# Weight preparation moved from GpSimd to VectorE, and a normalisation moved from the attention to the blocks' loads

## The chip, the cores and the metric

The kernel runs on one core of a Trainium2 chip. The metric is the device time of one execution in microseconds. Three executions of the kernel before took 843.49, 842.67 and 841.82 us; their median is 842.67 us. Engines are named as the profile names them: PE is TensorE (PEld its weight loads), DVE VectorE, ACT ScalarE, POOL GpSimd, and SP the engine that issues most transfers.

## What is computed

Three layers follow one another. The retention attention has 4 sequences of 576 tokens, 8 heads of 64. Its output, 2,304 tokens by 512 features, goes through a gated MLP with a root-mean-square normalisation in front, and the MLP's output goes to one of 8 experts per token, chosen by the first maximum of eight logits.

```python
scores = scale * q @ k.T;  ret = scores * Dmat          # Dmat[h,i,j] = gamma[h]**(i-j) for i >= j, else 0
x = (ret @ v).transpose(0, 2, 1, 3).reshape(2304, 512)
rms = sqrt(mean(x * x, -1) + 1e-6);  xn = x / rms * rms_g
y = silu(xn @ w_gate) * (xn @ w_val) @ w_out            # 512 -> 1536 -> 512
logits = y @ gate + modality_bias[modality_id]
out = softmax(logits)[e] * (relu(y @ w1[e]) @ w2[e])    # e = argmax, 512 -> 1024 -> 512
```

The gated MLP's weights arrive as 64-bit floating-point words. Each is brought to float32 and split into a high and a low part, and each product of the MLP is three matmuls (high by high, high by low, low by high).

## The kernel before, in words

The order of the work is written out by hand: each engine runs its instructions in the order in which the program emits them, and a tile's buffers (`bufs=`) are handed on when their last reader or writer is done.

**Attention** (lines 224 to 456). It goes in 20 steps, 5 chunks per sequence: four of 128 tokens and one of 64. In step g the loop of line 402 emits the loads of chunk g + 7 on SP, the decay of the next chunk's v on POOL (line 274), the scores of chunk g on PE (285) and their mask on DVE (289, two instructions), the sum of squares of chunk g − 3 on PE (348) with its square root on ACT (353), the state update (304, copied by ACT at 309 and 310), and the output of chunk g − 1 on PE (317 from the state, 324 from the chunk itself). DVE scales the output into the tile `x` (334), ACT squares it (336), and POOL adds the four squares of each token in two steps (338, 339). Four steps behind, `a_norm2` takes the reciprocal of the root on DVE (359) and multiplies x by it (360). Six steps behind, `a_store` (364) writes x to `xnd` in memory. The first 512 tokens, chunks 0 to 3, do not go through memory: `split_x` (198) splits them into the high and low parts of block 0 in steps 7 to 10 (DVE line 201, four instructions per chunk). The last three chunks stay in the tile `xlate` and are normalised and stored in steps 4 to 6 of block 0.

**Weight preparation.** `unpack` (127) treats one unit of 128 by 512 words in three stages. Stage 0 loads the raw words on SP (131). Stage 1 scales the low words on ACT (136), shifts the high words on DVE (137), merges two bit fields on DVE (140), and adds both as integers on POOL (143). Stage 2 rounds to the high part on ACT (147) and subtracts for the low part (148), on POOL or DVE as `lo_eng` says. `pipe` (174) staggers the units: a tick runs stage 1 of unit i, stage 2 of unit i − 2, and the load of a later unit. Five units are prepared in the attention from step 11 on, all on POOL. The other 30, with one more in two halves, are prepared beside block 0, three or four ticks a step, with `lo_eng` POOL for every second one.

**Gated MLP** (lines 735 to 848). Its blocks have 512, 512, 384, 384, 256 and 256 tokens, each in 12 steps of 128 hidden features. A step is 24 matmuls of gate and value (`gv_mm`, 212), the product on ACT and DVE (`gv_post`, 741: line 745 silu on ACT, 746 on DVE, 747 on ACT, 748 on DVE), and 3 matmuls for each chunk of the block (12 for four chunks) of the output projection of the step before (`out_acc`, 751). In block 0 the ticks of the weight preparation stand behind `gv_post`, so that in block 0 DVE runs lines 746 and 748 of a step and then that step's three or four units. A unit is needed by PE one or two steps later. `load_x` (187) brings the next block's x from `xnd` into the one buffer `xl`, in step 8 of block 0 and in step 2 of the others; at the end of a block `split_x` splits it. In blocks 1 to 5 DVE also routes the block before: line 767 forms a logit, with its unwanted products written to a corner of the tile `xl`.

**Experts** (line 850 to the end) are the same in both kernels.

Of the kernel before, what the change touches and what calls it, by code (L numbers as in the profile page):

```python
# [7 lines left out]
F32 = mybir.dt.float32  # L8
# [16 lines left out]
# tokens of the gated MLP's blocks: the first one hides the weight preparation, the last ones shorten the routing  # L25
# [3 lines left out]
NS0 = BLOCKS[0] // 128  # chunks that go to the first block without a trip to memory  # L29
XW = max(BLOCKS[1:])  # L30
CHUNKS = [(c * 128, min(128, S - c * 128)) for c in range(-(-S // 128))]
ROW = 528  # row of the experts' lists: features, logits, token
CAPS = [512, 512, 384, 320, 256, 256, 256, 256]  # static places by rank of an expert's count
EARLY = 256  # places of the first expert that are visited before the last block is routed
FILL = 512  # places of each list that are cleared
NL = 32  # most chunks beyond the static places
NWU = 13  # matmuls that wake the tensor engine's clock
QB = 8  # attention inputs in flight
XB = 10  # attention outputs in flight
SD = 6  # steps from an attention output to its store  # L40
# [15 lines left out]
def kernel(  # L56
# [39 lines left out]
    xnd = dram.tile([KD, 128, NT], F32, name="xnd")  # L96
    xs = dram.tile([E * NT, ROW], F32, name="xs")

# [1077 lines left out]
```

## Time and profile before

| What | us |
|---|---|
| median of three executions | 842.67 (841.82 to 843.49) |
| span of the profiled execution | 840.5 |
| PE busy | 802.7 (96%) |
| DVE busy | 523.0 (62%) |
| ACT busy | 291.1 (35%) |
| POOL busy | 181.7 (22%) |

The page gives the profiled execution as a span, from its first to its last instruction; the times of the executions are some 2 us longer. PE's busy time is an upper bound of its work, since matmuls overlap in the array and their ends are modelled. The start of one group of instructions to the start of the next is the safer measure of what a group takes. Shares over the whole span mix stages with different limits, so the stages have to be read one by one.

### The profile page before, as it was taken

The page shows a single profiled execution, that of the slowest core. Times are in us where ns is not written, and L with a number is a line of the kernel's source. Part 1 is how long each engine was busy: PE and PEld are TensorE (multiplying, and loading weights), DVE is VectorE, ACT ScalarE, POOL GpSimd, SP SyncE. Part 2 cuts the span into 40 slices and gives each one's busy share as a digit, 9 for nine tenths or more (in the row PEclk, how much of TensorE's full clock was granted, in tenths as well). Part 3 has the DMA queues.
Part 4 walks back from the last instruction along what each step waited for, and adds up shares of the span by engine and source line. Part 5 has one row for each costly group of instructions (what it writes and reads, how often), then busy time and mean ns, then how long its engine had stood idle before and what let it go on. Part 6 is the DMA issues. An engine that isn't in the chain of part 4 may idle for free.

```text
span 840.5 us, 13238 instructions
## 1 busy us (share of the span) xinstructions
PE 802.7 (96%) x5004; PEld 693.7 (83%) x5004; DVE 523.0 (62%) x1142; ACT 291.1 (35%) x567; POOL 181.7 (22%) x203
## 2 busy tenths in 40 slices
PE   8978988888999999999999999999999999999995
PEld 6867766656888889999999999999888898889894
DVE  3999799997454525654644475836575556576650
ACT  5443544344311113113111312124453344455540
POOL 4556766767000000010000001000100010011100
PEclk9998999999999999999999999999999999999998
DMA  9994463437930001000000100032635254776400
GB/s 322 338 328 169 148 246 109 134 109 253 325 129 27 1 13 51 15 26 14 26 14 13 32 21 26 14 130 110 212 142 189 89 194 149 271 265 226 147 19 12
DMA packets 47537, 106.29 MB, mean 126 GB/s; under 512 B 11182, under 2 KB 20398, under 8 KB 47344
## 3 DMA queue, kind: packets, MB, share of 16 engines
q1 hardware_dynamic: 43248, 95.32, 34.0%
q0 software_dynamic: 3168, 9.59, 3.0%
q8 instruction: 40, 0.66, 0.3%
q10 hardware_dynamic: 1056, 0.52, 0.2%
q14 instruction: 25, 0.20, 0.1%
HBM read 83.51 MB, written 22.82 MB: 127 GB/s over the span
## 4 chain that ended last, share of the span: by engine, by line
PE 77%; DVE 14%; issue 4%; DMA 2%; ACT 2%; POOL 1%; SPq 0%; another core or an unknown queue 0%; POOLq 0%; ACTq 0%; DVEq 0%
PE gv L208 10%; PE gv L210 10%; PE gv L209 10%; PE acc L208 10%; PE acc L209 9%; PE acc L210 9%; PE h L208 4%; PE h L209 4%; PE h L210 4%; DVE rawbt L137 3%; DVE rawbt L140 2%; DVE pt L289 2%; DVE w L148 1%; PE tp L723 1%; DVE x L360 1%
## 5 line engine op out<-in xcount | busy, mean ns | idle before, releaser
L210 PE MATMUL gv<-xh,w 128*128 128x512 f32 (+2 forms) x576 | 195.3, 339 | 7.9 <-POOL w L148 7.9
L208 PE MATMUL gv<-xh,w 128*128 128x512 f32 (+2 forms) x576 | 196.2, 341 | 2.6 <-ACT scratch L745 2.6
L209 PE MATMUL gv<-xo,w 128*128 128x512 f32 (+2 forms) x576 | 194.5, 338 | 0.0
L210 PEld LDWEIGHTS gv<-xh,w 128*128 128x128 f32 x576 | 109.3, 190 | 18.9 <-POOL w L148 11.1
L208 PEld LDWEIGHTS gv<-xh,w 128*128 128x128 f32 x576 | 109.5, 190 | 12.1 <-ACT scratch L745 3.0
L746 DVE TENSOR_TENSOR scratch<-gv,scratch 128x512 f32<-128x512 f32 (+2 forms) x72 | 40.0, 556 | 126.5 <-PE gv L210 126.5
L209 PEld LDWEIGHTS gv<-xo,w 128*128 128x128 f32 x576 | 109.4, 190 | 9.5
L747 ACT CAST hh<-scratch 128x512 fp32r<-128x512 f32 (+2 forms) x72 | 37.0, 514 | 177.2 <-DVE scratch L746 177.2
L676 DVE TENSOR_TENSOR w<-raw,w 128x1024 fp32r<-128x1024 f32 x64 | 78.1, 1225 | 26.1 <-ACT w L675 25.5
L767 DVE CUSTOM_DVE_ANT_0 xl<-row,wr 128x512 bf16<-128x512 f32 x128 | 88.2, 689 | 4.8 <-DMA xl<-xnd 2.2
L208 PE MATMUL h<-xt,w 128*128 128x256 f32 (+3 forms) x288 | 88.8, 308 | 0.0
L209 PE MATMUL acc<-wo,hh 128*128 128x512 f32 x216 | 85.6, 396 | 2.9 <-POOL wo L148 2.9
L208 PE MATMUL acc<-wo,hh 128*128 128x512 f32 x216 | 86.1, 399 | 2.3 <-ACT hh L747 2.3
L518 POOL DMA_INDIRECT xs<-row,sloti x16 | 18.0, 1127 | 320.8 <-DVE lg L767 173.6
L210 PE MATMUL h<-xt,w 128*128 128x256 f32 (+3 forms) x288 | 87.3, 303 | 0.0
L209 PE MATMUL h<-xt,w 128*128 128x256 f32 (+3 forms) x288 | 87.2, 303 | 0.0
L210 PE MATMUL acc<-wo,hl 128*128 128x512 f32 x216 | 85.6, 396 | 0.0
L745 ACT ACTIVATE scratch<-gv 128x512 f32<-128x512 f32 (+2 forms) x72 | 35.3, 491 | 143.5 <-PE gv L210 138.5
L893 POOL DMA_INDIRECT out_dram<-orow,idx x22 | 23.6, 1074 | 218.6 <-ACT ex L700 76.2
L748 DVE TENSOR_TENSOR hl<-scratch,hh 128x512 fp32r<-128x512 f32 (+2 forms) x72 | 40.8, 567 | 41.8 <-ACT hh L747 41.8
L675 ACT CAST w<-raw 128x1024 fp32r<-128x1024 f32 x64 | 66.0, 1043 | 1.5 <-DMA raw<-in_w_dram 1.5
L208 PE MATMUL acc<-w,rh 128*128 128x512 f32 (+1 forms) x160 | 63.6, 397 | 0.0
(216 smaller groups left out, 1352.7 us busy)
## 6 DMA issues: line engine op xcount, KB each, us to landing
raw<-in_w_dram SPq DMA_DIRECT2D x64, 512.0 KB, 4.9
rawb<-in_wgv_dram SPq DMA_DIRECT2D x20, 512.0 KB, 3.9
xs<-zero SPq DMA_DIRECT2D x8, 1056.0 KB, 13.3
qk<-in_qkt_dram SPq DMA_DIRECT2D x16, 512.0 KB, 7.9
vk<-in_vkn_dram SPq DMA_DIRECT2D x16, 512.0 KB, 9.4
rawb<-in_wout_dram SPq DMA_DIRECT2D x10, 512.0 KB, 3.6
rowc<-xs SPq DMA_DIRECT2D x19, 264.0 KB, 4.3
xnd<-x SPq DMA_DIRECT2D x8, 256.0 KB, 3.1
```

Source lines behind the costliest of these rows:

```text
L137: DVE.tensor_scalar(out=u, in0=hw, scalar1=3, scalar2=0x3FFFFFF8, op0=ALU.logical_shift_left, op1=ALU.bitwise_and)
L208: PE.matmul(ps, lh, rh, start=start, stop=False)
L209: PE.matmul(ps, lh, rl, start=False, stop=False)
L210: PE.matmul(ps, ll, rh, start=False, stop=stop)
L675: ACT.copy(out=w[:, 0, :], in_=raw)
L676: DVE.tensor_tensor(out=w[:, 1, :], in0=raw, in1=w[:, 0, :].bitcast(F32), op=ALU.subtract)
L745: ACT.activation(out=h, in_=gps[:, :n], func=ACTF.Silu)
L746: DVE.tensor_tensor(out=h, in0=vps[:, :n], in1=h, op=ALU.mult)
L747: ACT.copy(out=hh[:, :n], in_=h)
L748: DVE.tensor_tensor(out=hl[:, :n], in0=h, in1=hh[:, :n].bitcast(F32), op=ALU.subtract)
L767: DVE.tensor_tensor_reduce(out=junk, in0=row[:, 0:DM].rearrange("p (a b) -> p a b", a=2), in1=wr[:, e, :].rearrange("p (a b) -> p a b", a= ...
L893: POOL.indirect_dma_start(out=out[:, :], out_offset=bass.IndirectOffsetOnAxis(ap=idx[:m, i:i + 1], axis=0), in_=orow[:m, :], in_offset=Non ...
```

## The change

The weight preparation leaves POOL: lines 143 and 148 run on DVE for all units, and `lo_eng` is gone. The chunks behind the first block (4 to 19) are no longer normalised in the attention. They are stored as they come, three steps behind their output instead of six, all within the attention. Their sums of squares are gathered in four groups of 448 tokens (chunks 4 to 7, 8 to 11, 12 to 15, 16 to 19), one matmul and one square root per group, and the row of roots goes to a new array `rmsd` in memory. Each block loads its x one step (or, in block 0, five steps) away from where it did, in step 3, together with its row of roots spread over all partitions; from step 5 on DVE takes two reciprocals (half the tokens each) and two products (two of the four feature groups each), one instruction a step. In block 0 that row sits in the space of the router's weights `wr`, in the others in a row tile. The last chunk's sum of squares goes through POOL like the others. Comments were removed too.

```diff
-XB = 10  # attention outputs in flight
-SD = 6  # steps from an attention output to its store
+XB = 7
+SD = 3
-NLX = 3  # attention outputs normalised beside the first block
-LN = (4, 5, 6)  # the steps of the block that do so
-LP = 1  # last steps whose squares are summed on the tensor engine
+FX, FN = (3, 3), (5, 5)
+    rmsd = dram.tile([1, NT], F32, name="rmsd")
-    def unpack(src, hi, lo, raw, t, lo_eng):
+    def unpack(src, hi, lo, raw, t):
...
-            POOL.tensor_tensor(out=u, in0=u, in1=lw, op=ALU.add)
+            DVE.tensor_tensor(out=u, in0=u, in1=lw, op=ALU.add)
...
-            lo_eng.tensor_tensor(out=lo(), in0=u.bitcast(F32), in1=hi().bitcast(F32), op=ALU.subtract)
+            DVE.tensor_tensor(out=lo(), in0=u.bitcast(F32), in1=hi().bitcast(F32), op=ALU.subtract)
+    def norm_x(j, xl, rl):
+        t0, n = STARTS[j], BLOCKS[j]
+        rl = rl[:, :n]
+        SP.dma_start(out=rl, in_=rmsd[0:1, t0:t0 + n].to_broadcast([128, n]))
+        def inverse(o):
+            DVE.reciprocal(out=rl[:, o:o + n // 2], in_=rl[:, o:o + n // 2])
+        def scale(k):
+            DVE.tensor_tensor(
+                out=xl[:, k:k + 2, :n], in0=xl[:, k:k + 2, :n], in1=rl.unsqueeze(1).to_broadcast([128, 2, n]),
+                op=ALU.mult,
+            )
+        return [lambda: inverse(0), lambda: inverse(n // 2), lambda: scale(0), lambda: scale(2)]
...
-            if g < G - NLX:
-                x = att.tile([128, NP, 128], F32, tag="x", name="x", bufs=XB)
-            else:
...
+            x = att.tile([128, NP, 128], F32, tag="x", name="x", bufs=XB)
...
+            total = sq[:, 0, :n]
+            if g >= NS0:
+                gr, o = place[g]
+                if not o:
+                    sums[gr[0]] = att.tile([128, 512], F32, tag="sqs", name="sqs", bufs=2)
+                total = sums[gr[0]][:, o:o + n]
+            POOL.tensor_tensor(out=sq[:, 0:2, :n], in0=sq[:, 0:2, :n], in1=sq[:, 2:4, :n], op=ALU.add)
+            POOL.tensor_tensor(out=total, in0=sq[:, 0, :n], in1=sq[:, 1, :n], op=ALU.add)
...
         def a_norm1(g):
+            n, sq = steps[g][3], sq_t.pop(g)[:, 0, :]
+            if g >= NS0:
+                gr, o = place[g]
+                if g != gr[-1]:
+                    return
+                n, sq = o + n, sums.pop(gr[0])
+            ss = ps_g("ss")
+            PE.matmul(ss[:, :n], ones, sq[:, :n], start=True, stop=True)
...
+            if g < NS0:
+                ri_t[g] = ri
+            else:
+                b, c, o, _ = steps[gr[0]]
+                t0 = b * S + o
+                (ACT if g == G - 1 else SP).dma_start(out=rmsd[0:1, t0:t0 + n], in_=ri[0:1, :n])
...
-            q = ACT if G - NLX - LS <= g < G - NLX else SP
+            q = ACT if g >= G - LS else SP
...
-            if g >= NL2:
+            if NL2 <= g < NL2 + NS0:
                 a_norm2(g - NL2)
...
-                if j == 0 and f in LN:
-                    a_norm2(G - NLX + LN.index(f))
-                if j == 0 and f - 1 in LN:
-                    a_store(G - NLX + LN.index(f - 1))
-                if f == (LN[-1] + 2 if j == 0 else 2) and j + 1 < NB:
+                if f == FX[min(j, 1)] and j + 1 < NB:
                     x_in[:] = [load_x(j + 1)]
+                    norm = norm_x(j + 1, x_in[0], row_tile(F32, "rl") if j else wr[:, 0, :])
+                if j + 1 < NB and 0 <= f - FN[min(j, 1)] < len(norm):
+                    norm[f - FN[min(j, 1)]]()
```

## Rows read from the trace of the kernel before

**Rows 1.** Busy us by stage: PE, PEld, DVE, ACT, POOL; PE clock, DMA share, GB/s.

```profile
6.00:42.00 36.00, 34.47 (x511) 29.59 (x511) 26.10 (x40) 19.79 (x52) 19.42 (x25) 1.00 1.03 348
42.00:95.50 53.50, 42.96 (x557) 36.27 (x555) 51.63 (x82) 22.66 (x58) 32.92 (x39) 0.93 0.70 219
95.50:104.00 8.50, 8.50 (x39) 7.07 (x38) 4.71 (x7) 4.66 (x9) 7.38 (x7) 0.84 0.60 207
104.00:202.00 98.00, 82.30 (x338) 62.06 (x337) 90.54 (x98) 43.12 (x76) 65.37 (x42) 0.99 0.46 151
212.00:640.00 428.00, 427.96 (x2421) 380.90 (x2421) 234.39 (x693) 111.38 (x219) 29.13 (x56) 1.00 0.21 72
```

**Rows 2.** Waits of PE, 20 to 212 us: total, times, longest.

```profile
PE gv L210 <- POOL w L148: 7.9, 6, 1.9
PE st L304 <- POOL vk L274: 5.5, 6, 3.0
```

**Rows 3.** Timeline of PE, step 8 of the attention: start, us, line, operation.

```profile
34.38 1.16 PE L285 MATMUL sc<-qk 64*128 64x128 f32 x16
35.48 0.49 PE L348 MATMUL ss<-sq,ones 128*128 128x128 f32 x2
35.89 0.69 PE L304 MATMUL st<-vk 128*64 128x64 f32 x16
36.51 1.16 PE L317 MATMUL pv<-qk,sbd 128*128 128x128 f32 x8
37.60 1.09 PE L324 MATMUL pv<-pt,vk 128*64 128x128 f32 x16
38.62 0.68 PE L285 MATMUL sc<-qk 64*64 64x64 f32 x16
```

**Rows 4.** Timeline of DVE, step 7 of the attention and the start of step 8.

```profile
33.23 1.28 DVE L289 TENSOR_TENSOR pt<-sc,causal 128x512 f32<-128x512 f32 x2
34.50 0.69 DVE L334 TENSOR_TENSOR x<-pv,rc 128x512 f32<-128x512 f32 x1
35.11 0.94 DVE L359 RECIPROCAL ri<-ri 128x128 f32<-128x128 f32 x1
36.09 1.20 DVE L360 TENSOR_TENSOR x<-x,ri 128x512 f32<-128x512 f32 x1
37.22 2.11 DVE L201 SCALAR_TENSOR_TENSOR xo<-x,gt,xh 128x128 fp32r<-128x128 f32 x4
39.25 1.28 DVE L289 TENSOR_TENSOR pt<-sc,causal 128x512 f32<-128x512 f32 x2
```

**Rows 5.** Timeline of PE, the first matmul of block 0.

```profile
95.47 0.79 PE L208 MATMUL gv<-xh,w 128*128 128x512 f32 x1
```

**Rows 6.** Timeline of DVE in block 0: first step, a contended subtraction, tenth step.

```profile
103.73 0.69 DVE L746 TENSOR_TENSOR scratch<-gv,scratch 128x512 f32<-128x512 f32 x1 [3.73 <-PE gv L210]
...
105.72 0.42 DVE L137 TENSOR_SCALAR rawbt<-rawb 128x512 int32<-128x512 int32 x1
106.18 0.69 DVE L140 SCALAR_TENSOR_TENSOR rawbt<-rawb,rawbt 128x512 int32<-128x512 int32 x1
106.79 0.42 DVE L137 TENSOR_SCALAR rawbt<-rawb 128x512 int32<-128x512 int32 x1
...
110.97 0.68 DVE L148 TENSOR_TENSOR w<-rawbt,w 128x512 fp32r<-128x512 f32 x1
...
122.72 1.75 DVE L148 TENSOR_TENSOR w<-rawbt,w 128x512 fp32r<-128x512 f32 x1
...
202.27 0.68 DVE L746 TENSOR_TENSOR scratch<-gv,scratch 128x512 f32<-128x512 f32 x1
```

**Rows 7.** Groups by line, block 0, POOL's integer add: busy us, mean ns.

```profile
L143 POOL TENSOR_TENSOR rawbt<-rawbt,rawb 128x512 int32<-128x512 int32 x29 | 43.8, 1511 | 32.3 <-ACT rawb L136 12.4 <-DVE rawbt L140 9.2 <-ACT scratch L745 4.6
```

**Rows 8.** Timeline of POOL beside the contended subtraction of DVE.

```profile
122.21 1.71 POOL L148 TENSOR_TENSOR w<-rawbt,w 128x512 fp32r<-128x512 f32 x1
```

**Rows 9.** Waits of SP's queue, 0 to 215 us: total, times, longest.

```profile
SPq L131 <- POOL rawbt L143: 79.7, 21, 7.8
```

More of the change, by code (lines that the diff above doesn't have):

```diff
@@ L160, in once, with gv_unit @@
         return get
-    def gv_unit(u, raw, t, lo_eng):
+    def gv_unit(u, raw, t):
         f, i = divmod(u, 2)
@@ L170, in part @@
             return get
-        return unpack(wgv[f, i], part(0), part(1), raw, t, lo_eng)
+        return unpack(wgv[f, i], part(0), part(1), raw, t)
     def pipe(units, lead=2):
@@ L250 @@
         qk_t, vk_t, pt_t, x_t, sq_t, ri_t = {}, {}, {}, {}, {}, {}
-        late = []
+        groups, sums = [], {}
+        for g in range(NS0, G):
+            n = steps[g][3]
+            if not groups or sum(steps[i][3] for i in groups[-1]) + n > 512:
+                groups.append([])
+            groups[-1].append(g)
+        place = {g: (gr, sum(steps[i][3] for i in gr[:z])) for gr in groups for z, g in enumerate(gr)}
         def by_pair(ps):
@@ L336, in a_pv @@
             ACT.activation(out=sq[:, :, :n], in_=x[:, :, :n], func=ACTF.Square)
-            if g < G - LP:
-                POOL.tensor_tensor(out=sq[:, 0:2, :n], in0=sq[:, 0:2, :n], in1=sq[:, 2:4, :n], op=ALU.add)
-                POOL.tensor_tensor(out=sq[:, 0, :n], in0=sq[:, 0, :n], in1=sq[:, 1, :n], op=ALU.add)
+            total = sq[:, 0, :n]
[6 more added lines that the diff above has]
+            POOL.tensor_tensor(out=total, in0=sq[:, 0, :n], in1=sq[:, 1, :n], op=ALU.add)
             x_t[g], sq_t[g] = x, sq
         def a_norm1(g):
-            n = steps[g][3]
-            ss = ps_g("ss") if g < G - 2 else ps_o("ss")
-            sq = sq_t.pop(g)
-            parts = 1 if g < G - LP else NP
-            for p in range(parts):
-                PE.matmul(ss[:, :n], ones, sq[:, p, :n], start=(p == 0), stop=(p == parts - 1))
-            if g < G - NLX:
+            n, sq = steps[g][3], sq_t.pop(g)[:, 0, :]
[7 more added lines that the diff above has]
+            if g < NS0:
                 ri = att.tile([128, 128], F32, tag="ri", name="ri", bufs=3)
             else:
-                ri = late[0][:, g - G + NLX, NLX * 128:NLX * 128 + 128]
+                ri = att.tile([128, 512], F32, tag="rig", name="rig", bufs=2)
             ACT.activation(out=ri[:, :n], in_=ss[:, :n], func=ACTF.Sqrt, scale=1.0 / DM, bias=eps[:, 0:1])
-            ri_t[g] = ri
+            if g < NS0:
+                ri_t[g] = ri
[3 more added lines that the diff above has]
+                (ACT if g == G - 1 else SP).dma_start(out=rmsd[0:1, t0:t0 + n], in_=ri[0:1, :n])
         def a_norm2(g):
@@ L372, in unit_a @@
             t = once(lambda: att.tile([128, DM], I32, tag="rawt", name="rawt", bufs=3))
-            return gv_unit(u, raw, t, POOL)
+            return gv_unit(u, raw, t)
         def wo_unit_a():
@@ L378, in wo_unit_a @@
             wo[0] = w = once(lambda: w4_tile([128, 2, DM], F32R, "wo", True))
-            return unpack(wout[0], lambda: w()[:, 0, :], lambda: w()[:, 1, :], raw, t, POOL)
+            return unpack(wout[0], lambda: w()[:, 0, :], lambda: w()[:, 1, :], raw, t)
         prep_a = pipe([unit_a(u) for u in range(NUA)] + [wo_unit_a()], LD)
@@ L448 @@
                 split_x(x_t.pop(g - SX), xsp, 128 * (g - SX), 128)
-        for g in range(G + 1 - SD, G - NLX):
+        for g in range(G + 1 - SD, G):
             a_store(g)
@@ L472, in unit_b @@
         if kind == "gv":
-            return [gv_unit(u, raw, t, lo_eng)]
+            return [gv_unit(u, raw, t)]
         w = once(lambda: w4_tile([128, 2, DM], F32R, "wo"))
@@ L476, in unit_b @@
             wo[u] = w
-            return [unpack(wout[u], lambda: w()[:, 0, :], lambda: w()[:, 1, :], raw, t, lo_eng)]
+            return [unpack(wout[u], lambda: w()[:, 0, :], lambda: w()[:, 1, :], raw, t)]
         wo[u] = w
@@ L484, in unit_b @@
                 wout[u, :, i:i + 256], lambda i=i: w()[:, 0, i:i + 256], lambda i=i: w()[:, 1, i:i + 256],
-                raw, t, lo_eng,
+                raw, t,
             ))
@@ L784 @@
         ulist = []
-        for i, (kind, u) in enumerate(units):
-            ulist += unit_b(kind, u, POOL if i % 2 else DVE)
+        for kind, u in units:
+            ulist += unit_b(kind, u)
         prep_b = pipe(ulist)
```

5 lines of the change are left out of this document (1 added, 4 removed).

## The prediction

> **What bounds the kernel now.** I read the busy time by stage first [rows 1]. It shows three stages. From 42 to 95.5 us (the second half of the attention) and from 104 to 202 us (the first block of the gated MLP) DVE is busy 51.6 of 53.5 and 90.5 of 98 us while PE has holes; from 212 us on PE is busy 427.96 of 428 us. So time can be won only ahead of 212 us, and there only by work taken from DVE, or from whatever DVE waits for. The waits say the same of PE [rows 2]: its two longest waits are for POOL, 5.5 us for the decayed v of the attention and 7.9 us for weights' low parts, and POOL's one queue holds the weight preparation in both stages. Then the two chains in the attention: PE's own work of a full step takes 38.62 − 34.38 = 4.24 us, of which the sum of squares is 0.41 [rows 3]; DVE's of the step before it, with a normalisation and a split for block 0, 39.25 − 33.23 = 6.02 us [rows 4]. PE needs 8.26 us from the first matmul of block 0 to DVE's first product there [rows 5, 6], at a granted clock of 0.84, and DVE then needs 202.27 − 103.73 = 98.5 us for nine steps of the block [rows 6].
>
> **The change, part by part.** I go from stage to stage, with start-to-start times.
>
> Attention, steps 8 to 20. Removed from DVE: the reciprocal (0.98) and the multiply (1.13) of each chunk from 4 on [rows 4]. Steps 4 to 7 keep them, so nothing moves up to 39.25 us, when DVE starts the mask multiply of step 8. From there a step of DVE is mask 1.27 + output 0.61 + split 2.03 while the splits last (steps 8 to 10): 3.9 + 3.3 (64 tokens: half the mask) + 3.6 (half the output) gives 50.1. Steps 11 to 19 are mask and output: six full at 1.88, the two of 64 tokens at 1.26 and the one behind the first of them at 1.57, 15.4 us. Into them come five weight units. Each takes on DVE the shift 0.46 and the merge 0.61 as now, and new an integer add and a subtraction. The subtraction is 0.60 as DVE's own [rows 6]. The add is on no row of DVE: below it stands 0.46 (one int32 input, same shape), above it 1.51, which POOL takes for it [rows 7]. I take 0.61, that of the merge, which also reads two int32 tiles of this size on DVE. Four and a half units of 2.28 are 10.3 us. 50.1 + 15.4 + 10.3 = 75.8; the routing constants, unchanged, come on top, for which I put 3 (an estimate: one and a half full steps' masks and outputs), about 79.
>
> PE over the same time: the mask of step 10 ends at 39.25 + 3.9 + 3.3 + 1.27 = 47.7 and its output matmuls (1.02) at 48.7. Steps 12 to 20 are six full ones (3.83 without the sum of squares), less 1.09 where a sequence begins, half the scores and half an output at each chunk of 64 tokens, and two group sums of 448 columns (between 0.41, one chunk, and 1.44, 3.5 chunks; I take 1.0): 30.4 us, so 79.1. The transfers: 36 × 348 GB/s and 53.5 × 219 GB/s moved 24.2 MB from 6 to 95.5 us, and three chunks' stores (0.64 MB) come in from block 0; at 348 GB/s that is 71 us, to about 77. Three chains near 79 will not pass without stops: where PE and DVE were close, PE lost 1.5 of 36 us [rows 1], which is 1.6 of these 40.
>
> Here row and rule part. DVE's subtraction took 0.68 at 110.97 us and 1.75 at 122.72 us [rows 6], 1.07 more; the second one ran beside a subtraction of POOL that had begun at 122.21 us [rows 8]. The attention keeps POOL busy with decays and sums, and nine adds and subtractions on two inputs come to DVE there; if each met POOL, 9.6 us; at a quarter of them, 2.4. So 79 + 1.6 + 2.4 = 83 for the end of the attention, between 79 and 90, where 95.5 stood. The Trainium skill (SBUF — State Buffer, Who interferes with whom) says that a DVE instruction with two SBUF inputs and a GpSimd instruction that reads SBUF lock each other out for a whole instruction. By that rule the move pays in block 0, where POOL falls idle, and costs in the attention; the sum by it alone would take the 90.
>
> The stores come three steps after the output instead of six, and three more of them, with three of the four root-mean-square rows, are issued by SP inside the attention. What stands behind them on SP is the raw weights. SP spent 79.7 us waiting for raw tiles that POOL held [rows 9]; that wait covers the issues. Without it, raw weights land late, ACT's conversion and DVE's shift wait, and the masks queued behind them: a part of the 90.
>
> Entry of block 0: 8.26 us at a clock of 0.84 are 7.0 at full clock, if PE's holes behind POOL are gone; the group's sum takes the place of the single chunks' sums. DVE's first product comes at 83 + 7 = 90.0 instead of 103.7. It also waits for ACT, which now issues the last stores and the last row ahead of the block's activation: nothing while two passes of matmuls hide it, otherwise about a microsecond.
>
> Block 0, nine steps of DVE: product to first shift 105.72 − 103.73 = 1.99 [rows 6], nine times 17.9; 30 units' shift, merge and add 1.68 each, 50.4; 28 subtractions 16.8; the next block's normalisation, two reciprocals of 256 columns at 1.96 (twice 128) and two products of 1,024 elements at 1.2 (twice the subtraction), 6.3. Together 91.4 against 98.5, bounds 86 (add 0.46, half the normalisation) and 95 (a POOL-free price of the add 0.12 higher). Three late chunks' normalisation, some 5 us, is what the 6.3 replaces. So the tenth product stands at 181.4 instead of 202.3, and PE, which then has 72 matmuls of the block ahead of it as before, ends 20.9 us earlier. PE's own nine steps are about 36 matmuls each and shorter (it had 82.3 busy of 98 us), so DVE still sets the pace.
>
> Blocks 1 to 4. Four normalisations of the block after come to DVE, four instructions each, and a load of x one step later with a row spread over the partitions beside it on SP. Priced as above, 384 columns cost 4.7 and 256 cost 3.2: 15.8 us in all, against 234 of 428 us busy [rows 1]. I cost them at nothing, covered by PE's one step of lookahead; without cover they are 15.8 us.
>
> The sum is −13.7 − 7.1 = −20.8: span 840.5 becomes 819.7. The median, 842.67, is 2.2 above the profiled span; I keep that and predict 822.0.
>
> **The rivals.** *Contention and late raw weights take the attention's part.* For: DMA at a share of 1.03 up to 42 us [rows 1] and the 1.75 beside 0.68. Against: only nine such instructions. The attention ends at 90, the gain is 13.8, and the time 829. The Trainium skill's rule of the shared ports (SBUF — State Buffer, Who interferes with whom) would be the mechanism; the trace's 1.75 agrees with it, and no run shows yet how often it strikes in the attention.
>
> *Slower: the integer add is dear on DVE.* It decides in block 0, where DVE has no slack: each 0.1 us more costs 3 us in 30 units. At 0.61 + 20.8/30 = 1.30 all is given back; at POOL's 1.51 the loss is 27 of which 20.8 are paid, 842.67 + 6 = 849. For: no row shows it. Against: the merge, two int32 inputs, at 0.61.
>
> *The normalisation stalls the later blocks.* For: it is queued on DVE ahead of the products that PE waits for, and the blocks of 256 tokens give it the shortest steps to hide in. If half of 15.8 us came through, 830. Against: PE has no hole from 212 to 640 us [rows 1].
>
> *No gain*: raw weights, not DVE, become the pace of both stages, so that the time stays at 842. Against: in block 0 DMA has a share of 0.46 [rows 1].
>
> **How the numbers follow.** The forecast, DVE relieved in both stages, has 0.72. Contention has 0.10, stalls in later blocks 0.06, no gain 0.05, the dear add 0.07. The forecast's own bounds: 79 for the attention and 86 for the block give −30 and 812; 90 and 95 give −10.2 and 832. The range 813 to 833 takes in the first three cases but for their edges, about 0.82. Faster by over 0.2% (1.7 us, about what a measurement of this kernel can tell from no change) is the sum of these three, 0.88; same 0.05; slower 0.07.
>
> **What would show it.** Right: the first product of block 0 near 90 us and the tenth near 181; POOL without work from there to the block's end; shift, merge, add and subtraction at 0.4 to 0.7 each; PE without waits for POOL's weights; PE still full from 190 us on. Wrong: an add far above 0.7, which overthrows block 0; subtractions and adds near 1.7 in the attention, or ACT and DVE waiting there for raw tiles, which overthrows the 83; holes of PE behind DVE in the blocks of 384 and 256 tokens, which overthrow the zero. If DVE reached 79 as summed and PE did not, the term that failed is the handing over between them.

## The result and the profile after

The changed kernel takes 832.65 us, the median of four runs (831.01 to 836.12); the kernel before took 843.08 on the same chip (841.82 to 846.14). The ratio is 0.9876, with a 95% interval of 0.9857 to 0.9895: 10.4 us faster where 20.7 were forecast. The profiled execution took 832.61 us with a span of 830.8.

Busy time by stage of the changed kernel, columns as in [rows 1], with the edges moved to where its stages now begin:

```profile
6.00:42.00 36.00, 34.10 (x505) 28.95 (x504) 25.16 (x38) 19.03 (x49) 19.35 (x24) 1.00 1.02 336
42.00:86.00 44.00, 37.76 (x540) 31.23 (x536) 35.24 (x66) 20.38 (x48) 24.94 (x33) 1.00 0.92 290
86.00:97.00 11.00, 8.71 (x34) 6.18 (x30) 4.57 (x9) 5.75 (x9) 2.88 (x4) 0.84 0.81 291
97.00:194.00 97.00, 84.86 (x348) 64.98 (x346) 85.66 (x141) 42.27 (x76) 0.00 (x0) 0.98 0.45 146
212.00:640.00 428.00, 427.96 (x2425) 381.33 (x2424) 247.78 (x710) 109.20 (x216) 29.89 (x56) 1.00 0.19 67
```

The second half of the attention shrank from 53.5 to 44 us; DVE is busy 35.2 of those 44 and no longer fills them, while the DMA share rose from 0.70 to 0.92. The entry of block 0 (86 to 97) got longer, with the clock still at 0.84. In block 0 POOL has no work at all. Behind 212 us PE is as full as before (427.96 of 428) with 13.4 us more of DVE beside it: the later blocks' normalisation costs nothing, as forecast.

Waits of PE (total, times, longest), first from 42 to 97 us, then from 97 to 194; they answer to [rows 2]:

```profile
PE st L327 <- POOL vk L297: 3.4, 3, 1.4
PE ss L374 <- POOL sqs L362: 3.1, 2, 2.3
...
PE acc L224 <- ACT hh L778: 6.8, 4, 2.3
PE acc L225 <- DVE wo L147: 4.3, 4, 1.5
```

The wait for POOL's weights is gone, and in block 0 PE waits for ACT and DVE instead; the wait for the decayed v is not gone, and POOL's sum of squares now stands in the entry.

DVE in the attention of the changed kernel (start, us, line, operation, idle time before it); it answers to [rows 4]:

```profile
42.47 2.47 DVE L217 SCALAR_TENSOR_TENSOR xo<-x,gt,xh 128x128 fp32r<-128x128 f32 x4 [1.38 <-ACT xh L216]
...
47.19 2.47 DVE L217 SCALAR_TENSOR_TENSOR xo<-x,gt,xh 128x128 fp32r<-128x128 f32 x4 [0.99 <-ACT xh L216]
...
52.02 2.06 DVE L217 SCALAR_TENSOR_TENSOR xo<-x,gt,xh 128x128 fp32r<-128x128 f32 x4 [0.83 <-ACT xh L216]
...
65.32 0.69 DVE L352 TENSOR_TENSOR x<-pv,rc 128x512 f32<-128x512 f32 x1 [2.00 <-PE pv L347]
65.92 0.17 DVE L470 CAST mf<-m 128x18 f32<-128x18 int32 x1
```

In [rows 4] the split follows the normalisation without idle time. With the normalisation gone, DVE comes to the split before ACT has its rounded part: 1.38 + 0.99 + 0.83 = 3.2 us of waits in steps 8 to 10. The last two lines (output of step 13, then the routing mask's cast, which finds its load landed) are taken up below.

The entry of block 0, timelines of PE, ACT and DVE; it answers to [rows 5, 6]:

```profile
86.11 0.51 PE L224 MATMUL gv<-xh,w 128*128 128x512 f32 x1
...
91.46 1.73 PE L374 MATMUL ss<-sqs,ones 128*128 128x448 f32 x2 [2.29 <-POOL sqs L362]
92.31 1.31 PE L224 MATMUL gv<-xh,w 128*128 128x512 f32 x1
...
93.23 0.63 ACT L379 ACTIVATE rig<-ss,eps 128x448 f32<-128x448 f32 x1 [1.99 <-PE ss L374]
...
94.40 1.28 ACT L776 ACT_TABLE_LOAD   x1 [0.54 <-ACT rig L379]
95.70 0.60 ACT L776 ACTIVATE scratch<-gv 128x512 f32<-128x512 f32 x1
...
96.97 0.69 DVE L777 TENSOR_TENSOR scratch<-gv,scratch 128x512 f32<-128x512 f32 x1 [5.00 <-PE gv L226]
```

From first matmul to first product 10.86 us, where 8.26 stood and 7.0 was forecast. PE runs out of matmuls at 89.2 and waits for the last chunk's sum. Ahead of the wait its granted clock is 1.00 (86.0 to 89.2) and a matmul's record is 0.39 to 0.40 long; behind it the clock is 0.51, near the lower level of 1.2 GHz, until 95.1, and three full records there are 0.63 long.

One weight unit of block 0 on DVE, and the tenth product; it answers to [rows 6]:

```profile
109.77 0.42 DVE L136 TENSOR_SCALAR rawbt<-rawb 128x512 int32<-128x512 int32 x1
110.22 0.69 DVE L139 SCALAR_TENSOR_TENSOR rawbt<-rawb,rawbt 128x512 int32<-128x512 int32 x1
111.05 0.69 DVE L142 CUSTOM_DVE_ANT_0 rawbt<-rawb,rawbt 128x1024 uint16<-128x1024 uint16 x1
111.66 0.68 DVE L147 TENSOR_TENSOR wo<-rawbt,wo 128x512 fp32r<-128x512 f32 x1
112.26 0.42 DVE L136 TENSOR_SCALAR rawbt<-rawb 128x512 int32<-128x512 int32 x1
...
193.96 0.68 DVE L777 TENSOR_TENSOR scratch<-gv,scratch 128x512 f32<-128x512 f32 x1
```

The add, a custom operation on halfwords here, is 0.69 us long, and the next instruction follows 0.61 behind it, the price that was taken. But it starts 0.83 behind the merge, where the price was the 0.61 from a merge to the instruction that followed it then [rows 6].

That block 0 got shorter at all, with 141 instructions on DVE where 98 stood, has its reason in the other instructions. Groups of DVE by line (busy us, mean ns, idle time before) in block 0, shift and merge, first of the kernel before (104 to 202 us), then of the changed kernel (97 to 194 us):

```profile
L137 DVE TENSOR_SCALAR rawbt<-rawb 128x512 int32<-128x512 int32 x30 | 27.0, 899 | 0.0
L140 DVE SCALAR_TENSOR_TENSOR rawbt<-rawb,rawbt 128x512 int32<-128x512 int32 x30 | 31.8, 1059 | 1.0
```

```profile
L136 DVE TENSOR_SCALAR rawbt<-rawb 128x512 int32<-128x512 int32 x30 | 12.6, 421 | 0.0
L139 DVE SCALAR_TENSOR_TENSOR rawbt<-rawb,rawbt 128x512 int32<-128x512 int32 x30 | 20.8, 692 | 1.0
```

With POOL idle these two take 25.4 us less, which pays for the 30 adds (20.8 us busy). In norm_only below, where POOL keeps the preparation, they are 863 and 1059 ns long.

The profiled executions in milestones (us); the ratio is to the kernel before on the same chip:

| kernel | first matmul of block 0 | first product | tenth product | span | median | ratio and interval |
|---|---|---|---|---|---|---|
| before | 95.47 | 103.73 | 202.27 | 840.5 | 843.08 | |
| forecast | 83 | 90.0 | 181.4 | 819.7 | 822.0 | |
| changed | 86.11 | 96.97 | 193.96 | 830.8 | 832.65 | 0.9876 [0.9857, 0.9895] |
| norm_only | 85.94 | 98.13 | 196.89 | 834.4 | 836.83 | 0.9935 [0.9916, 0.9954] |
| prep_only | 101.48 | 111.23 | 206.86 | 843.3 | 843.83 | 1.0013 [0.9999, 1.0027] |
| add_apart | 87.80 | 97.56 | 188.23 | 825.1 | 826.74 | 0.9809 [0.9793, 0.9825] |
| add_or | 86.47 | 95.84 | 191.89 | 830.9 | 831.10 | 0.9855 [0.9838, 0.9871] |
| chain_apart | 84.90 | 95.32 | 182.04 | 820.8 | 820.88 | 0.9736 [0.9717, 0.9755] |
| v0_first | 87.61 | 99.84 | 197.21 | 836.4 | 833.18 | 0.9888 [0.9872, 0.9905] |
| last_first | 85.99 | 94.17 | 191.20 | 829.5 | 831.86 | 0.9867 [0.9850, 0.9883] |
| last_pe | 86.42 | 94.69 | 191.83 | 829.8 | 831.84 | 0.9866 [0.9850, 0.9881] |
| no_sums | 83.25 | 90.93 | 187.97 | 872.5 | 875.71 | 1.0388 [1.0355, 1.0420] |
| split_early | 85.32 | 96.19 | 193.19 | 829.7 | 830.54 | 0.9843 [0.9810, 0.9876] |
| mask_early | 86.37 | 95.77 | 192.79 | 830.9 | 832.66 | 0.9862 [0.9844, 0.9881] |
| split_mask | 82.63 | 91.76 | 188.76 | 827.2 | 828.28 | 0.9819 [0.9796, 0.9842] |
| all3 | 85.75 | 94.25 | 184.93 | 821.9 | 823.67 | 0.9774 [0.9754, 0.9793] |
| all4 | 83.58 | 91.50 | 178.26 | 815.8 | 817.66 | 0.9698 [0.9683, 0.9713] |
| all5 | 82.80 | 92.87 | 179.80 | 818.3 | 820.05 | 0.9702 [0.9677, 0.9728] |

(The profiled execution of v0_first is the longest of its five, 838.38 us, so its column of times is no term of its median.)

Ahead of the tenth product the changed kernel misses the forecast by 12.6 us: 3.1 at the end of the attention, 3.9 in the entry, 5.6 in block 0. Its span misses by 11.1 only: from the tenth product to the end it takes 636.8 us where the kernel before took 638.2, and most of that lies ahead of the twelfth product (10.3 against 11.4 us). Milestones are read from one execution each, and such readings differ: mask_early, whose time is that of the changed kernel, has its first product 1.2 us earlier and its twelfth 0.4 us later. The experiments take these three in turn, after one pair on the parts of the change.

### The profile page after: what moved, and what is told of

Its sections match the earlier page's. It is cut to its first block, busy times and chain, and to the rows that moved or that the text cites. A ratio compares the mean times of both kernels' runs of the same rounds, so it can differ in the third digit from the quotient of the medians.

```text
span 830.8 us, 13136 instructions
## 1 busy us (share of the span) xinstructions
PE 796.8 (96%) x4974; PEld 687.9 (83%) x4974; DVE 514.9 (62%) x1187; ACT 288.2 (35%) x555; POOL 98.2 (12%) x148
## 4 chain that ended last, share of the span: by engine, by line
PE 76%; DVE 14%; issue 4%; ACT 2%; DMA 2%; POOL 1%; SPq 0%; another core or an unknown queue 0%; DVEq 0%; POOLq 0%; ACTq 0%
PE gv L224 10%; PE gv L225 10%; PE gv L226 10%; PE acc L224 10%; PE acc L226 10%; PE acc L225 10%; PE h L224 5%; PE h L225 4%; PE h L226 4%; DVE rawbt L139 2%; DVE rawbt L142 2%; DVE w L147 2%; DVE rawbt L136 1%; DVE pt L312 1%; PE tp L754 1%
## 5 line engine op out<-in xcount | busy, mean ns | idle before, releaser
L224 PE MATMUL acc<-w,rh 128*128 128x512 f32 (+1 forms) x160 | 63.7, 398 | 0.0
L225 PE MATMUL acc<-w,rh 128*128 128x512 f32 (+1 forms) x160 | 63.3, 396 | 0.0
L226 PE MATMUL acc<-w,rl 128*128 128x512 f32 (+1 forms) x160 | 63.3, 395 | 0.0
```

The costliest lines, as they stand in the source:

```text
L224: PE.matmul(ps, lh, rh, start=start, stop=False)
L225: PE.matmul(ps, lh, rl, start=False, stop=False)
L226: PE.matmul(ps, ll, rh, start=False, stop=stop)
```

## The experiments

**Which part pays.** norm_only keeps the weight preparation of the kernel before in the changed one; prep_only gives the kernel before the changed preparation and nothing else.

```diff
norm_only
-            DVE.tensor_tensor(out=u, in0=u, in1=lw, op=ALU.add)
+            POOL.tensor_tensor(out=u, in0=u, in1=lw, op=ALU.add)
-            DVE.tensor_tensor(out=lo(), ...
+            lo_eng.tensor_tensor(out=lo(), ...
prep_only: the same lines the other way round, in the kernel before
```

> The normalisation part alone: sums by group, division at the block's load, but the weight preparation as in the kernel before (POOL's add, every second subtraction on POOL). Theory (the normalisation is the part that pays, because the attention was bound by DVE): the first product of block 0 stands at 93 to 97 as in the changed kernel, block 0 stays at 98 to 99 from the first to the tenth product, and the time is 832 to 836, nearly all of the gain. Rival (each part relieves DVE or what DVE waits for, and both pay, as predicted): without the preparation's part POOL's adds hold up the decay and the weights, the first product stands at 99 or later, and the time is 837 to 841.

> The preparation part alone: the kernel before with the integer add and all subtractions on DVE, attention outputs normalised as before. Theory: in the attention the five units lay 4 to 10 us on DVE, which has nothing free there, so that the first product moves from 103.7 to 106 to 112; block 0 shrinks by 1 to 3 us only, because the add starts 0.82 behind the merge; the time is 843 to 850, equal to or slower than the kernel before. Rival (POOL was what both stages waited for): the first product stays at 103 to 104, block 0 shrinks by 3 us or more, and the time is 836 to 840.

norm_only gained 0.65%, prep_only nothing that the runs can tell from no change. Alone, their first products move by −5.6 and +7.5 us, their block 0 by +0.2 and −2.9. Together the first product moves by −6.8 and block 0 by −1.5. So the theory holds for prep_only: where DVE is full, the five units of the attention put the first matmul of block 0 6.0 us later (101.48 against 95.47); where the normalisation has made room, their additions and subtractions on DVE cost nothing (86.11 with them, 85.94 without). norm_only came out between theory and rival, 836.83: the attention relieved as in the theory, and POOL's preparation still slowing block 0. The parts are worth more together than apart: −10.4 us against −6.3 + 0.7 = −5.6.

**Block 0: the add's late start.** add_apart puts the add of unit i behind the subtraction of unit i−2; add_or leaves it where it is and makes it a plain bitwise operation; chain_apart also parts shift and merge.

```diff
add_apart, per tick
     units[i][1]()          # shift, merge
     units[i - 2][2]()      # subtraction
+    units[i][3]()          # add
add_or
-            DVE.tensor_tensor(out=u, in0=u, in1=lw, op=ALU.add)
+            DVE.tensor_tensor(out=u, in0=u, in1=lw, op=ALU.bitwise_or)
chain_apart, per tick
     units[i][1]()          # shift
+    units[i - 1][4]()      # add
+    units[i][3]()          # merge
     units[i - 2][2]()      # subtraction
```

> The integer add of a weight unit is emitted behind the subtraction of the unit two before, so that it no longer follows its own merge directly. Theory handing-over (the add starts 0.82 us after the merge instead of 0.61 because it waits until the merge is through): 0.2 us less per unit, 28 units, so the stretch from the first to the tenth product of block 0 falls from 97.0 to about 91.3 us and the time by about 5.5 us. Rival price (the add's instruction costs this gap wherever it stands): 97.0 stays and the time stays at 832.6.

> The integer add is replaced by a bitwise or of the same two tiles (the carry out of the rounding is left out). If the gap of 0.2 us ahead of the add belongs to the form in which the add runs on this engine, the or starts 0.61 us after the merge, the stretch from the first to the tenth product of block 0 falls from 97.0 to about 91 us, and the time by about 6 us. If it belongs to the wait for ACT's conversion or to the merge's result, the or starts 0.8 us after the merge and the time stays.

> The changed kernel with the three integer steps of a weight unit apart from each other on DVE: shift of unit i, add of unit i-1, merge of unit i, subtraction of unit i-2. Theory (a DVE instruction that reads what the one directly ahead of it wrote starts late, the add behind the merge by 0.2 us and the merge behind the shift by 0.1): the next instruction starts 0.34 to 0.37 behind a shift where it was 0.45, and 0.60 behind each of the other three; first to tenth product 87 to 88 us where it was 97.0; time 822.5 to 825. Rival (only the add is held, by a wait of its own): 0.45 behind the shift stays, first to tenth product 90 to 91, time 826 to 827.5, as with the add alone apart.

DVE in block 0 of add_apart:

```profile
110.36 0.69 DVE L139 SCALAR_TENSOR_TENSOR rawbt<-rawb,rawbt 128x512 int32<-128x512 int32 x1
110.97 0.69 DVE L150 TENSOR_TENSOR wo<-rawbt,wo 128x512 fp32r<-128x512 f32 x1
111.57 0.69 DVE L145 CUSTOM_DVE_ANT_0 rawbt<-rawb,rawbt 128x1024 uint16<-128x1024 uint16 x1
112.17 0.42 DVE L136 TENSOR_SCALAR rawbt<-rawb 128x512 int32<-128x512 int32 x1
```

DVE in chain_apart, first the block's first unit, which has no add to put between, then a later one:

```profile
97.36 0.42 DVE L136 TENSOR_SCALAR rawbt<-rawb 128x512 int32<-128x512 int32 x1
97.81 0.69 DVE L142 SCALAR_TENSOR_TENSOR rawbt<-rawb,rawbt 128x512 int32<-128x512 int32 x1
...
106.23 0.42 DVE L136 TENSOR_SCALAR rawbt<-rawb 128x512 int32<-128x512 int32 x1
106.56 0.69 DVE L148 CUSTOM_DVE_ANT_0 rawbt<-rawb,rawbt 128x1024 uint16<-128x1024 uint16 x1
107.17 0.69 DVE L142 SCALAR_TENSOR_TENSOR rawbt<-rawb,rawbt 128x512 int32<-128x512 int32 x1
107.77 0.68 DVE L153 TENSOR_TENSOR wo<-rawbt,wo 128x512 fp32r<-128x512 f32 x1
```

With another instruction between, the add starts 0.60 behind its neighbour, and block 0 takes 90.7 us from first to tenth product, which is the forecast's 91.4. The plain operation, also 0.69 long, still starts 0.80 behind the merge and block 0 stays at 96.1, so the custom form is the cause of 0.03 at most. In chain_apart the step behind a shift falls from 0.45 to 0.33 where something stands between, and stays 0.45 in the one unit where nothing does; block 0 takes 86.7. The theory's numbers came out, and the rival (a wait of the add's own) falls: in these chains a DVE instruction that reads, and writes over, what the one directly ahead of it wrote starts late, 0.2 us behind a merge and 0.1 behind a shift. The operand from ACT is not it: add_apart's add has it too, and for the add at 111.05 ACT was done at 109.71. How the engine holds the start is not shown. The Trainium skill (VectorE: DVE Perf Modes, The DRAIN you can't avoid) says of eight copies in a row that a semaphore (the signal that an instruction waits for) after each of them costs nothing extra. No run here takes only a semaphore away; what they show is that the order counts: the same four operations per unit, reordered, take 10.3 us less over 30 units.

**The entry.** v0_first issues the second pass of block 0 ahead of the last group's sum; last_first puts the last weight unit of the attention behind the last output; last_pe sums the last chunk's squares by matmuls; no_sums takes POOL's sums away from chunk 4 on and so leaves out three quarters of each of these sums of squares.

```diff
v0_first
         g0 = gv_mm(0, 0, xsp, BLOCKS[0])
+        v0 = gv_mm(0, 1, xsp, BLOCKS[0])
         a_norm1(G - 2)
         a_norm1(G - 1)
-        v0 = gv_mm(0, 1, xsp, BLOCKS[0])
last_first
-            if g >= PA:
+            if g >= PA and g != G - 1:
                 next(prep_a, lambda: None)()
+            if g == G:
+                next(prep_a, lambda: None)()
last_pe
+            if g < G - 1:
+                POOL.tensor_tensor(...)      # both sums
...
+            for p in range(NP if g == G - 1 else 0):
+                PE.matmul(ss[:, m:n], ones, sq4[:, p, :n - m], start=(p == 0), stop=(p == NP - 1))
no_sums, chunks from 4 on
-            ACT.activation(out=sq[:, :, :n], in_=x[:, :, :n], func=ACTF.Square)
-            POOL.tensor_tensor(...)
-            POOL.tensor_tensor(...)
+                ACT.activation(out=total, in_=x[:, 0, :n], func=ACTF.Square, scale=2.0)
```

> The second pass of block 0's first 24 matmuls (value) is put ahead of the last group's sum of squares, so that PE no longer waits for POOL between the two passes (2.29 us in the changed kernel) and keeps its clock. Theory PE (PE's wait and the slow clock behind it set the entry of block 0): DVE's first product of block 0 moves from 96.97 us to about 93, and the time falls by 3 to 4 us. Rival ACT (the root of the last sum, the store that ACT issues, and the load of the Silu table stand ahead of block 0's first activation, and the root still waits for POOL's sum): the first product moves to about 95.5, and the time falls by 1 to 2 us.

> The weight preparation of attention step 19 goes behind the last chunk's output instead of ahead of it, nothing else. If the last output is late because it stands on DVE behind a weight unit (shift, merge, add, subtraction: 85.98 to 89.06 us in the changed kernel), then output, square and sums come about 2.9 us earlier, PE's wait of 2.29 us ahead of the last sum goes, the clock of block 0's value matmuls stays at full, and the first product is near 93 us instead of 96.97: 3 to 4 us off the time. If POOL's sums themselves or ACT's table load set the entry, the first product moves by less than 1.5 us.

> The changed kernel with the squares of the last chunk (64 tokens) summed by four accumulating matmuls, so that POOL's two sums are out of the chain ahead of the last group's root. Theory (the entry of block 0 lasts 10.9 us instead of 7.0 because the last output passes ACT's squares, POOL's sums of 1.8 us, the group's matmul, the root and the table load): PE's wait of 2.3 us falls to 0.8 to 1.2, the first product moves from 97.0 to 95 to 96, the time to 831 to 832.2. Rival (the lower clock of PE that follows the wait is the cost, and a shorter wait with more matmuls behind it leaves it): the first product stays at 96.5 to 97.5 and the time at 832.2 to 833.2.

> The changed kernel without POOL's sums of squares for chunks from 4 on: ACT squares the first 128 features only and writes them where the sum was written (three quarters of the sum of squares of those chunks are left out). Theory (the attention of the changed kernel loses time where the decay of v stands behind sums on POOL's queue, 4.9 us of DVE's waits, and at its end 2.3 us of PE's): the first matmul of block 0 moves from 86.1 to 81 to 83.5, the first product from 97.0 to 90 to 93.5, the time to 826 to 830; the preparation's add and subtraction in the attention stay at 0.72 to 0.88 and 0.9. Rival (POOL's sums lengthen DVE's own instructions): these two fall to 0.6 to 0.7 each and the mask multiply below 1.27, with the waits of DVE for PE as they were.

The entry of v0_first, timelines of PE, ACT and DVE:

```profile
95.79 0.91 PE L374 MATMUL ss<-sqs,ones 128*128 128x448 f32 x2
...
97.92 1.28 ACT L776 ACT_TABLE_LOAD   x1 [0.54 <-ACT rig L379]
...
99.84 0.69 DVE L777 TENSOR_TENSOR scratch<-gv,scratch 128x512 f32<-128x512 f32 x1 [6.83 <-ACT scratch L776]
```

v0_first gained nothing, not even the 1 to 2 us of the rival: PE no longer waits, but the sum is later, and ACT takes root, store and table load, in this order, ahead of the first activation. The chain that sets the entry is last output, ACT's square, POOL's two sums, PE's sum, ACT's root, store, table load, activation; the second pass must be through as well. In the changed kernel that pass came last, in v0_first ACT's activation. The expectation that PE's wait was the whole cost fell. What shortens that chain pays at the first product: −2.8 in last_first, −2.3 in last_pe (−1.6 and −1.1 if mask_early is the measure), and the clock of the entry is 1.00 in both. Of this 0.1% is left in the time (the intervals overlap with the changed kernel's). At the end of block 0 PE falls to the lower clock in both. Busy time by stage of last_first, one stretch, and then the same of last_pe:

```profile
194.00:198.00 4.00, 4.00 (x13) 3.10 (x13) 3.62 (x8) 1.25 (x4) 1.10 (x3) 0.64 0.96 405
```

```profile
194.00:198.00 4.00, 4.00 (x11) 3.19 (x12) 3.66 (x10) 1.76 (x5) 1.10 (x3) 0.59 1.01 422
```

In the changed kernel the clock is 1.00 in that stretch. 0.36 and 0.41 of 4 us are 1.4 and 1.6 us, and from the tenth to the twelfth product both take 11.8 us where the changed kernel takes 10.3: 1.5 us are lost again. The shorter chain is not shown to be the reason, since mask_early and add_or, which leave that chain as it is, have clocks of 0.67 and 0.57 there and the same 11.8.

In no_sums the entry takes 90.93 − 83.25 = 7.7 us at a clock of 1.00: PE's two passes with the sum between them take 6.9, the forecast's 7.0, and ACT's activation comes 0.8 behind. (Its span is not read: 685 us follow its tenth product, 637 in the changed kernel, presumably because other factors send other tokens to the experts.) It also shows what POOL's sums do to DVE. Groups of DVE instructions by line, 40 to 105 us (busy us, mean ns, idle time before), of the changed kernel:

```profile
L217 DVE SCALAR_TENSOR_TENSOR xo<-x,gt,xh 128x128 fp32r<-128x128 f32 x12 | 7.0, 640 | 3.2 <-ACT xh L216 3.2
L142 DVE CUSTOM_DVE_ANT_0 rawt<-raw,rawt 128x1024 uint16<-128x1024 uint16 x5 | 4.2, 836 | 1.3 <-ACT raw L135 1.1
L147 DVE TENSOR_TENSOR w<-rawt,w 128x512 fp32r<-128x512 f32 x4 | 3.5, 879 | 1.1 <-ACT w L146 1.1
```

and of no_sums:

```profile
L217 DVE SCALAR_TENSOR_TENSOR xo<-x,gt,xh 128x128 fp32r<-128x128 f32 x12 | 3.7, 353 | 2.0 <-ACT xh L216 2.0
L142 DVE CUSTOM_DVE_ANT_0 rawt<-raw,rawt 128x1024 uint16<-128x1024 uint16 x5 | 3.5, 693 | 0.7
L147 DVE TENSOR_TENSOR w<-rawt,w 128x512 fp32r<-128x512 f32 x4 | 2.7, 687 | 0.8 <-ACT w L146 0.8
```

The theory has the milestones of the attention, the rival the lengths: these waits shrink (the load of the routing mask takes 4.2 us back), and DVE's split, add and subtraction get shorter (the mask multiply, which reads scores from PSUM, does not). Add and subtraction fall to the lengths that they have in block 0, where POOL is idle. Their share is 0.7 + 0.8 = 1.5 us, in the place of the 2.4 estimated; the splits' is 3.3, and in the kernel before, with 604 ns, they were nearly as long as in the changed one. The Trainium skill (SBUF — State Buffer, Who interferes with whom) has a DVE instruction with two SBUF inputs contend with a GpSimd instruction that reads SBUF, and calls the shared ports an exclusive lock. The trace agrees that they slow each other, but the changed kernel's add at 74.20 us took 0.87 where 0.69 is its length alone, beside POOL sums of 0.85 (from 73.66) and 0.79 (from 74.59): the records overlap, and 0.18 is far from a whole instruction.

**The end of the attention.** split_early issues ACT's part of the split ahead of the step's output; mask_early issues the load of the routing mask at step 8; split_mask does both.

```diff
split_early
+            if 0 <= g - SX < NS0:
+                split_hi(x_t[g - SX], xsp, 128 * (g - SX), 128)
             if g >= 1:
                 a_pv(g - 1)
mask_early
-            if g == 11:
+            if g == 8:
                 SP.dma_start(out=m64, ...
```

> The changed kernel with ACT's part of the split for block 0 (the rounded copy) issued ahead of the step's output, DVE's part where it was. Theory (DVE waits 3.2 us for that copy in steps 8 to 10, in the place of the removed normalisation): these waits fall under 0.7 us together, the first matmul of block 0 moves from 86.1 to 83 to 84.5, and the time to 829.5 to 831.5. Rival (the chain through POOL's decay and PE sets the attention's end, so that the stop only moves on): DVE's wait for PE in steps 12 and 13 grows by as much, the first matmul stays at 85.5 to 86.5, and the time at 832 to 833.5.

> The changed kernel with the load of the routing mask and bias issued at step 8 of the attention instead of 11. Theory (in the changed kernel DVE arrives just when the mask has landed, held up by the split's waits and by PE): no wait is removed, the first matmul of block 0 stays at 85.5 to 86.5 and the time at 831.5 to 833.5. Rival (the mask's load already delays the changed kernel): the first matmul comes 1 us or more earlier and the time is 831 or less.

> The changed kernel with ACT's part of the split early and the mask's load at step 8. Theory (with the split's waits gone, only that load, landing at 65.3 us, held DVE): DVE's wait of 5.4 us is gone, the first matmul of block 0 comes at 82.5 to 84, the time is 827.5 to 829.5. Rival (the transfers as a whole pace the attention, with a DMA share over 1 from 42 to 72 us): the next inputs are late in the mask's place, the first matmul stays at 84.8 to 85.8, the time at 830 to 831.5.

split_early, timelines of SP's queue and of DVE:

```profile
57.92 0.33 SPq L476 DMA_DIRECT2D m<-in_mod_dram  x1
...
59.24 0.69 DVE L359 TENSOR_TENSOR x<-pv,rc 128x512 f32<-128x512 f32 x1 [2.00 <-PE pv L354]
65.32 0.18 DVE L479 CAST mf<-m 128x18 f32<-128x18 int32 x1 [5.38 <-DMA m<-in_mod_dram]
```

split_mask, timelines of DVE and PE:

```profile
65.23 0.43 DVE L136 TENSOR_SCALAR rawt<-raw 128x512 int32<-128x512 int32 x1 [2.63 <-DMA raw<-in_wgv_dram]
...
82.63 0.79 PE L231 MATMUL gv<-xh,w 128*128 128x512 f32 x1
```

With the split's waits gone DVE was 6.1 us ahead (the output that stood at 65.32 in the changed kernel is at 59.24), and gave 5.4 back to a load of 18 KB that was issued at 57.92 and landed 7.4 us later. So split_early's first matmul, at 85.32, came between theory and rival, and its time (830.54) is not told apart from the changed kernel's. In the changed kernel the same cast runs at 65.92 without a wait: DVE came just then, so that wait was hidden behind the others, and mask_early alone moved nothing (ratio 0.9862). Without both, the first matmul comes at 82.63, the forecast's 83, and the ratio falls to 0.9819 from 0.9843 (these two overlap; split_mask and the changed kernel do not). The rival is right about what is next: the raw weights, 2.6 us late.

**All together.** all3 joins last_first, add_apart and split_early; all4 joins last_first, chain_apart, split_early and last_pe; all5 adds the mask's early load.

> The changed kernel with three edits at once: the last weight unit of the attention behind the last output, the add of unit i behind the subtraction of unit i-2, and ACT's part of the split ahead of the step's output. Theory (three separate terms): the first product at 92 to 94, first to tenth product 90 to 91, the time 821 to 824, the sum of the separate gains being 0.8 + 5.9 + 2.1 = 8.8. Rival (they share the same slack): 825 to 827, no better than the add apart alone by more than 1.5 us.

> All edits that bear on the steps of the prediction that missed: last weight unit behind the last output, the three integer steps apart, ACT's part of the split early, the last chunk's squares summed on PE. Theory (separate terms): the first product at 90 to 93, first to tenth product 87 to 91, the time 817 to 822, about where the prediction put the changed kernel. Rival (the end of block 0 or raw weights take over): PE or DVE wait for raw tiles in block 0, and the time is 822 to 826.

> The four edits taken together before (weight unit behind the last output, integer steps apart, early split on ACT, last squares on PE) and the mask's load at step 8. Theory: 1 to 2.5 us less than the four alone, 815 to 816.7, with the first product at 89 to 90.5. Rival (transfers pace the attention): 817 to 818.5, the first product at 91 to 92.

all3 and all4 came out at the sum of their parts, to half a microsecond: 832.65 − 8.8 = 823.85 against 823.67, and 832.65 − (11.8 + 2.1 + 0.8 + 0.8) = 817.15 against 817.66. all4 has the lowest median and beats both kernels, by 3.0% and 1.8%. all5 is not told apart from it (817 to 821 us in its five runs): in its profiled execution the first matmul is 0.8 us earlier, but the first product 1.4 later. The trace shows what took it. Busy time of the stretch from 82 to 93 us, all4 and then all5:

```profile
82.00:93.00 11.00, 10.62 (x63) 8.66 (x63) 7.52 (x13) 6.51 (x11) 1.53 (x2) 1.00 0.82 299
```

```profile
82.00:93.00 11.00, 11.00 (x51) 8.89 (x50) 5.64 (x10) 5.89 (x9) 1.26 (x2) 0.72 0.80 284
```

PE's granted clock is 0.72 in all5's entry, PE having waited 1.8 us for POOL's sum ahead of the last chunk's output matmuls. Over its five executions the mean clock goes with the time: 816.5 and 817.0 us at 0.993 and 0.992, 820.1 to 821.1 at 0.988 to 0.990, where all4's five have 0.993 and 0.994. So these runs show no gain of the mask's early load on top of the rest.

## Why the prediction was half right

**Right.** DVE bound both stages and the time was won there; the shift, merge, add and subtraction are 0.42, 0.69, 0.69 and 0.69 long once POOL is idle; a product's 1.98 us to the first shift against 1.99; the later blocks cost nothing (626.6 us from the twelfth product to the end, 626.8 before); contention in the attention, 1.5 us against 2.4. The prices of shift and merge were right because they were taken from rows without POOL beside them; the 25.4 us that this saves in block 0 carried the forecast, and its sum does not name them.

**Luck.** The measured 832.65 lies inside the range of 813 to 833, at its edge, but not for the range's reasons: block 0 took 97.0 us where 86 to 95 were allowed, and the entry's 7.0 had no bounds. What the range had kept for the attention (90, where 86.1 was measured) happened to cover most of both.

**Block 0, the 91.4.** The step that failed is "The add is on no row of DVE ... I take 0.61, that of the merge". The 0.61 was a step from the merge to an instruction that does not need it [rows 6]; the add needs it, and starts 0.83 behind. Shift, merge and add of a unit take 0.45 + 0.83 + 0.61 = 1.89 where 1.68 was put, and 0.21 × 30 = 6.3 us; the normalisation, at 5.6 instead of 6.3, gives 0.7 back, and 5.6 are missing. The rival of the dear add had the place right and the mechanism not: its price lies in its neighbour, and the shift and merge of the kernel before had paid 0.1 us of the same kind all along.

**Entry, the 7.0.** The step "if PE's holes behind POOL are gone; the group's sum takes the place of the single chunks' sums" failed in its second half. The kernel before had no hole in its entry (PE busy 8.50 of 8.50 us [rows 1]); its clock was low there from the first matmuls on, whose records are 0.63 long until 98.2 us. The first pass of the changed kernel did run at full clock. But a new hole opened behind it: before, the last chunk's squares were summed on PE; now they pass POOL, behind a weight unit of DVE that holds up the last output, and PE waits 2.29 us and comes out of it at a clock of 0.51. With POOL's sums gone PE's two passes take 6.9 us and the entry 7.7, the rest being ACT's root, store and table load, put at "nothing while two passes of matmuls hide it".

**Attention, the 83.** The step "mask 1.27 + output 0.61 + split 2.03" failed: it took the split as ready when DVE was, though it reads ACT's part, for which the removed normalisation had been the cover; and "the routing constants, unchanged, ... for which I put 3" priced their instructions and not their load, which landed at 65.3 us, 7.4 after its issue, while the DMA share was 1.09 (57.9 to 65.3 us in split_early); what made it that slow is not shown. Each hid the other in the changed kernel. With both waits removed the first matmul comes at 82.63, but not because the terms were right: in split_mask DVE waits 5.6 us for PE's outputs and 2.6 for raw weights, where 1.6 were put for all stops, and the splits and the constants' instructions (1.2 us where 3 were put) take less than the sum had. That the two cancel is luck.

**The parts.** The sum was made for the whole change, and no step of it said that the preparation alone gains nothing. The normalisation has to leave the attention first, to make room on DVE for what the preparation brings there.

## What to carry to other kernels

When an instruction is removed ahead of another on a busy engine, ask which of the other's inputs were late and hidden behind it, and price a moved instruction by its distance to the one it reads from, not by its length alone. On DVE, steps of independent tiles set between the steps of one chain are worth as much here (10 us) as the whole change. And a wait found in a trace is worth only the distance to the next one: remove both in one run before the term is called wrong.

## What was not expected of the hardware

A DVE instruction directly behind its producer starts 0.12 us (merge behind shift, 0.45 against 0.33) to 0.22 us (add behind merge, 0.83 against 0.61) later than an instruction that needs nothing from the one ahead. A shift of 128 by 512 int32 on DVE, which has one input only, took 0.90 us on average beside POOL's preparation in block 0 and 0.42 with POOL idle. An int32 add on DVE runs as an operation on 1,024 halfwords, 0.69 us for 512 words, as long as the bitwise one. PE's granted clock at the end of block 0 is not the same in all runs: from 194 to 198 us it is 1.00 in the changed kernel, where PE had been busy 3.04 of the 4 us ahead, and 0.64 in last_first, where it had been busy 1.81; from its tenth to its twelfth product last_first takes 1.5 us longer.
